# Lower halves of the experts' second weights computed ahead of the expert part and kept in DRAM

## The chip, the cores and the metric

The kernel runs on one core of a Trainium2 chip. The metric is the time of one execution on the device in microseconds (us); a version is judged by the median of its runs. A profile is one further execution with the hardware profiler on.

## What is computed

Three stages follow one another. The reference, cut to what matters here:

```python
a = exp(phi - max); a = a / sum(a)                       # memory slots, softmax over the sequence
k_m, v_m = a^T k, a^T v                                  # 8 x 8 heads, 32 slots of 64
x = softmax(q k_m^T / 8) v_m                             # 4608 tokens, 512 wide
x = max(x @ w1, x @ w2, x @ w3) @ w_out                  # 512 -> 768 -> 512
logits = x @ w_gate                                      # 8 experts
# tokens in order of their best logit take an expert, each expert takes at most 576 tokens
for e in range(8):
    h = maximum(x[mask_e] @ moe2_w1[e], 0)               # 512 -> 1024
    out[mask_e] = h @ moe2_w2[e]                         # 1024 -> 512
```

## The kernel before

TensorE multiplies each pair of matrices as three products of rounded float32 numbers: every operand is split in a high part (a rounded copy, made by ScalarE) and a low part (what the copy lost, made by a subtraction on VectorE or GpSimd), and high times high, high times low and low times high are added up in PSUM. The page's names are PE (TensorE), ACT (ScalarE), DVE (VectorE), POOL (GpSimd) and SP (the sync engine, which here issues nearly all loads and stores).

The first part works on four units of two batches each (1152 tokens). A unit has the attention, then `layer1` (L588 to L606: 72 steps of six products into one of three `acc` buffers in PSUM; the first of each three steps is read out by ACT, L604, the other two by DVE, L606), then `layer2` (L646 to L676, written to the DRAM tensor `x2s`). The weights of layer 1 are folded with the unit's `v_m` by `fold` (L560 to L584) from pieces `wr` that SP loads (L554). The order of unit 0 is a list written by hand (`ORDER`); in the units 1 to 3 the loop at the end of the kernel (L1208 to L1235) emits one step of `layer1` or `layer2` after another and lets the object `flow` put the steps of the next unit's attention between them. Layer 2 of the last six tiles of unit 2 and of all of unit 3 is put off into the stretch behind the units. `consts` (L1101) builds some thirty small tables for the routing, in a pool `route`, as steps of `flow`; in the kernel before it is called near the end of unit 0 (entry `X` of the list), so that its instructions run at the start of unit 1.

The second part takes the experts one after another. For each, routing finds the 576 tokens: small instructions on DVE with small products on PE between them, six digits of a search and then `close`, `ties`, `places` and `index` (L740 to L945), emitted through `flow` in the midst of the matmuls of the expert before. POOL gathers the tokens (`xg`, L988), PE transposes them, `l1` (L1023 to L1039, 16 steps of twelve products of 288 columns) makes the hidden layer, which ACT (L1038) and DVE (L1039) read out, and `l2` (L1048 to L1071) makes the output, which POOL scatters. The expert's weights come through four buffers `wa` of 512 KB, loaded by SP at the expert's number. `split1` (L1006) splits a first weight: `ah` by ACT (L1010), `al` by POOL (L1011). `split2` (L1014) splits an eighth of the second weight: `bh` by ACT (L1020), `bl` by POOL (L1021). So POOL makes 64 pieces of `al` and 64 of `bl`, each a subtraction of 128 x 512 numbers with both inputs in SBUF; the pieces of `bl` are emitted in the second half of an expert's `l1`.

All engines run their own instructions in the order in which they are emitted; a DMA that SP issues waits in that order too.

Of the kernel before, what the change touches and what calls it, by code (L numbers as in the profile page):

```python
# [77 lines left out]
def staged(f):  # L78

    def whole(*x):  # L80
        for _ in f(*x):
            pass
    whole.stages = f
    return whole
# [57 lines left out]
def moe_kernel(tc, q, k, v, phi, w1, w2, w3, w_out, w_gate, m_w1, m_w2, out):  # L142
# [15 lines left out]
    with ExitStack() as ctx:  # L158
        def pool(name, bufs=1, **kw):
            return ctx.enter_context(tc.tile_pool(name=name, bufs=bufs, **kw))  # L160
# [384 lines left out]
                G.tensor_tensor(wol[:, x, :DM], dst, woh[:, x, :DM].bitcast(F32), op=OP.subtract)  # L545

        halves = [(u, i, a) for u in range(NU) for i in range(NF) for a in range(2)]
        WR = 4  # L550
# [83 lines left out]
        @staged  # L634
        def split_h(u, t, c):
            hT = st["hT", u][:, 3 * c:3 * c + 3, 128 * t:128 * t + 128]
            hh = wp.tile([128, 3, 128], F32R, name="hh", bufs=3)
            hl = wp.tile([128, 3, 128], F32R, name="hl", bufs=3)
            st["h", u, t, c] = hh, hl
            A.activation(hh, hT, AF.Copy)  # L640
            yield
            V.tensor_tensor(hl, hT, hh.bitcast(F32), op=OP.subtract)
# [335 lines left out]
        def done(j):  # L978
            if j == 1:
                free[0] += 1  # L980
                wload()
# [31 lines left out]

        def split2(ph, m):  # L1014
            h, j = divmod(m, 2)
            if m == 0:
                st["w2"] = [mp.tile([128, FE // 128, DM], F32R, name=s, bufs=1) for s in ("bh", "bl")]
            r = st["raw", ph, "b", h][:, j]
            hi, lo = (x[:, m] for x in st["w2"])
            A.activation(hi, r, AF.Copy)  # L1020
            G.tensor_tensor(lo, r, hi.bitcast(F32), op=OP.subtract)  # L1021
            done(j)

        def l1(ph, m, h, k):
            xh, xl = st["xT"]
# [74 lines left out]

        def consts():  # L1101
            nonlocal before, onesb, row, rowb, lanef, vals, em8, em8b, me8, thr0, times, OH, reach, some, number, part, remR, asg, ucap, upper, lower, code, where, zero, Lm, am8, me, rp
            unit0.close()
            rp = pool("route", side="right")
            later = Later(V=V, G=G)

# [75 lines left out]
        for u in range(NU):  # L1182
            if u == 0:
                table = dict(lp=lambda b: load_phi(0, b), lpr=lambda: load_phr(0), lk=lambda n: more(load_kv, kvs),
                             lkr=lambda: load_kvr(0), ld=lambda n: load_d("w"), lo=lambda n: load_d("o"),
                             lq=lambda n: more(load_q, qs), lg=load_g, c=staged(lambda n: conv.stages("w", *divmod(n, 2))),
                             d=staged(lambda n: conv.stages("o", n)), g=gate_a, G=gate_b, X=consts, H=lambda *x: split_h(*x), M=layer2,
                             L=staged(lambda i, b, h, w: layer1.stages(0, i, b, h, w)))
                for n in range(2):
                    attT_steps(n)  # L1190
                    steps = dict(att_steps(n), T=st["T", n], f=staged(lambda i, g, n=n: fold.stages(n, i, g)))
                    table.update({"1" * n + x: f for x, f in steps.items()})
                live = {}
                for x in ORDER.split():
                    name, *x = x.replace("!", "").split(".")
                    x = tuple(int(y) for y in x)
                    f = table[name]
                    if name[-1] == "f" and (name, x) not in live:

                        for y in live:  # L1200
                            if y[0][-1] == "f":
                                for _ in live[y]:
                                    pass
                    if hasattr(f, "stages"):
                        next(live.setdefault((name, x), f.stages(*x) if (name, x) not in live else None), None)
                    else:
                        f(*x)
            else:  # L1208
                if u + 1 < NU:
                    flow.add(att_steps(u + 1))  # L1210
                    flow.spread(2.9 * 4 * NF)
                for i in range(NF):
                    for n in range(4):
                        for w in range(3):
                            flow.main(lambda: main1(u, i, n, w), 0.75 + 0.5 * (w == 0))
                flow.flush()
            if u == NU - 1:
                last_logits(u, NF - 1)
                last_logits2(u)
                break  # L1220
            if u == 0:
                continue
            flow.add(attT_steps(u + 1))

            nt = NT if u < NU - 2 else 3
            flow.spread(4.0 * nt)
            for t in range(nt):
                for i in range(NF):
                    if (t, i) in ((0, 3), (2, 3)):
                        fold(u + 1, 0, t // 2)  # L1230
                    flow.main(lambda: layer2(u, t, *divmod(i, 3)), 0.67)
            flow.flush()
            if u == NU - 2:
                attention.close()
                hp = pool("last", side="right")  # L1235
        phase1.close()
        mp = pool("moe")
# [39 lines left out]
        for ph in range(E):  # L1277
            more_ = ph + 1 < E
            runs = [(m, h) for m in range(FE // 128) for h in range(2)]
            if ph == 0:  # L1280

                runs[1:3] = runs[2:0:-1]
                for t in range(3):
                    x_steps(0)[t][0]()
            for n, (m, h) in enumerate(runs):
                if h == (ph == 0) and m + 2 < FE // 128:
                    split1(ph, m + 2)
                if m >= 4:
                    split2(ph, 2 * (m - 4) + h)
                for k in range(4):  # L1290
                    flow.main(lambda: l1(ph, m, h, k), 0.37)
                if ph == 0 and n < 2:
                    x_steps(0)[n + 3][0]()
            gathered = 0
            for t in range(5):
                if t in (1, 2):
                    half(ph, t - 1)
                for m in range(FE // 128):
                    if more_ and not gathered and (("si", ph + 1) in st and t or (t, m) == (3, 0)):
                        ready(ph + 1)  # L1300
                        gathered = t + 1
                    if more_ and (t, m) in ((3, 2), (3, 6)):
                        split1(ph + 1, m // 4)
                    flow.main(lambda: l2(ph, t, m), 0.65 if t < 4 else 0.43)
                    at = (0, 1, 2, 3, 4) if gathered < 4 else (1, 3, 5, 6, 7)
                    if more_ and t == 4 and m in at:
                        x_steps(ph + 1)[at.index(m)][0]()
# [25 lines left out]
```

## Time and profile before

| | before |
|---|---|
| median of 3 runs | 1166.09 us (1165.29 to 1168.97) |
| the profiled execution | 1170.43 us, its span 1168.7 us |
| PE busy | 1067.4 us (91% of the span) |
| DVE busy | 679.3 us (58%) |
| ACT busy | 397.2 us (34%) |
| POOL busy | 334.7 us (29%) |
| bytes moved by DMA | 127.75 MB, 109 GB/s over the span |

Unit 0 ends at 219 us, unit 1 at 357 us, unit 2 at 466 us and unit 3 at 546 us after the span's start; the first expert's products begin at 631 us. Shares of the whole span mix these stages, so the rows further down are taken by stage. A row that says what an engine waited for names the instruction that came last.

### The profile page before, as it was taken

The page shows a single profiled execution, that of the slowest core. Times are in us where ns is not written, and L with a number is a line of the kernel's source. Part 1 is how long each engine was busy: PE and PEld are TensorE (multiplying, and loading weights), DVE is VectorE, ACT ScalarE, POOL GpSimd, SP SyncE. Part 2 cuts the span into 40 slices and gives each one's busy share as a digit, 9 for nine tenths or more (in the row PEclk, how much of TensorE's full clock was granted, in tenths as well). Part 3 has the DMA queues.
Part 4 walks back from the last instruction along what each step waited for, and adds up shares of the span by engine and source line. Part 5 has one row for each costly group of instructions (what it writes and reads, how often), then busy time and mean ns, then how long its engine had stood idle before and what let it go on. Part 6 is the DMA issues. An engine that isn't in the chain of part 4 may idle for free.

```text
span 1168.7 us, 21288 instructions
## 1 busy us (share of the span) xinstructions
PE 1067.4 (91%) x8426; PEld 909.2 (78%) x8426; DVE 679.3 (58%) x1690; ACT 397.2 (34%) x879; POOL 334.7 (29%) x361
## 2 busy tenths in 40 slices
PE   4688999999999999999996898998989789899996
PEld 3477799878998888777775778887777777779895
DVE  6798844764636456434573768677694865822120
ACT  2454344424343334223332323242231412324240
POOL 2123210120101001000003545535454424556462
PEclk8799999999999999999997999999989989899999
DMA  9964545337211521200132332423232222333311
GB/s 289 314 203 141 171 120 170 96 105 226 86 69 59 154 78 46 76 16 10 55 127 77 108 113 60 140 69 119 78 120 91 80 66 91 109 113 115 111 59 40
DMA packets 103763, 127.75 MB, mean 109 GB/s; under 512 B 18928, under 2 KB 79344, under 8 KB 103664
## 3 DMA queue, kind: packets, MB, share of 16 engines
q1 hardware_dynamic: 95184, 102.80, 28.7%
q0 software_dynamic: 5888, 18.88, 5.1%
q10 hardware_dynamic: 2592, 4.72, 1.1%
q8 instruction: 66, 1.08, 0.4%
q14 instruction: 33, 0.27, 0.1%
HBM read 102.78 MB, written 23.59 MB: 108 GB/s over the span
## 4 chain that ended last, share of the span: by engine, by line
PE 35%; DVE 11%; issue 3%; POOL 2%; ACT 1%; another core or an unknown queue 1%; DMA 0%; POOLq 0%
PE acc L1036 12%; PE acc L1059 12%; PE acc L667 5%; PE acc L1063 2%; DVE reach L739 1%; PE tr L1000 1%; PE fold L755 1%; DVE hT L1039 1%; POOL bl L1021 1%; PE fold L939 1%; DVE gs L801 0%; DVE gx L804 0%; ACT hT L1038 0%; DVE wol L1003 0%
## 5 line engine op out<-in xcount | busy, mean ns | idle before, releaser
L600 PE MATMUL acc<-ah,Wh 128*128 128x288 f32 x576 | 180.6, 313 | 4.9 <-DVE hT L606 4.2
L1059 PE MATMUL acc<-bh,hT 128*128 128x512 f32 x512 | 173.0, 406 | 6.3 <-DVE hT L1039 6.3
L1036 PE MATMUL acc<-woh,ah 128*128 128x288 f32 x512 | 163.9, 320 | 10.0 <-DVE hT L1039 8.9
L600 PE MATMUL acc<-ah,Wl 128*128 128x288 f32 x576 | 169.7, 295 | 1.2 <-DVE Wl L584 1.2
L600 PE MATMUL acc<-al,Wh 128*128 128x288 f32 x576 | 169.9, 295 | 0.0
L1036 PE MATMUL acc<-wol,ah 128*128 128x288 f32 x512 | 158.1, 309 | 0.2
L1036 PE MATMUL acc<-woh,al 128*128 128x288 f32 x512 | 156.9, 306 | 0.0
L600 PEld LDWEIGHTS acc<-ah,Wh 128*128 128x128 f32 x576 | 108.1, 188 | 36.8 <-DVE hT L606 16.1
L606 DVE TENSOR_TENSOR hT<-hT,acc 128x288 f32<-128x288 f32 x192 | 85.8, 450 | 79.7 <-PE acc L600 72.0
L1059 PEld LDWEIGHTS acc<-bh,hT 128*128 128x128 f32 x512 | 97.6, 191 | 29.2 <-DVE hT L1039 7.0
L1036 PEld LDWEIGHTS acc<-woh,ah 128*128 128x128 f32 x512 | 102.6, 200 | 22.4 <-DVE hT L1039 10.4
L600 PEld LDWEIGHTS acc<-ah,Wl 128*128 128x128 f32 x576 | 108.1, 188 | 1.4 <-DVE Wl L584 1.4
L600 PEld LDWEIGHTS acc<-al,Wh 128*128 128x128 f32 x576 | 108.3, 188 | 0.1
L1038 ACT ACTIVATE hT<-acc 128x288 fp32r<-128x288 f32 x128 | 52.7, 412 | 151.0 <-PE acc L1036 141.5
L1011 POOL TENSOR_TENSOR al<-wa,ah 128x512 fp32r<-128x512 f32 x64 | 83.9, 1318 | 69.4 <-ACT ah L1010 69.0
L1036 PEld LDWEIGHTS acc<-wol,ah 128*128 128x128 f32 x512 | 102.7, 201 | 1.0 <-DVE wol L1003 0.7
L1036 PEld LDWEIGHTS acc<-woh,al 128*128 128x128 f32 x512 | 102.7, 201 | 0.0
L1059 PE MATMUL acc<-bl,hT 128*128 128x512 f32 x256 | 101.8, 398 | 0.0
L1021 POOL TENSOR_TENSOR bl<-wa,bh 128x512 fp32r<-128x512 f32 x64 | 85.7, 1364 | 34.3 <-ACT bh L1020 34.1
L1039 DVE SCALAR_TENSOR_TENSOR hT<-acc,hT 128x288 fp32r<-128x288 f32 x128 | 56.6, 453 | 64.5 <-ACT hT L1038 64.0
L988 POOL DMA_INDIRECT xg<-x2s,gi x40 | 41.0, 1025 | 179.9 <-DVE some L763 168.2
L1067 ACT ACTIVATE o<-acc 128x512 f32<-128x512 f32 (+1 forms) x40 | 23.9, 598 | 198.3 <-PE acc L1059 141.4
(263 smaller groups left out, 2076.6 us busy)
## 6 DMA issues: line engine op xcount, KB each, us to landing
wa<-in_moe_w_dram SPq DMA_DIRECT2D x64, 512.0 KB, 3.6
wr<-ws SPq DMA_DIRECT2D x36, 384.0 KB, 3.0
dw<-in_moe_w_dram SPq DMA_DIRECT2D x36, 256.0 KB, 4.7
q<-in_q_dram SPq DMA_DIRECT2D x7, 1024.0 KB, 5.5
kv<-in_k_dram SPq DMA_DIRECT2D x27, 256.0 KB, 4.3
kv<-in_v_dram SPq DMA_DIRECT2D x27, 256.0 KB, 4.6
ws<-wr SPq DMA_DIRECT2D x12, 384.0 KB, 2.9
x2s<-xs ACTq DMA_DIRECT2D x18, 256.0 KB, 2.0
```

What stands on the lines that cost most here:

```text
L600: PE.matmul(p, x[:, b, g, f], y[:, g, c], start=(n == 0), stop=(n == 5))
L606: V.tensor_tensor(o, o, p, op=OP.max)
L667: PE.matmul(p, x[:, j], y[:, i, width * a:width * a + width], start=(i == 0 and m == 0), stop=(i == NF - 1 and m == 2))
L988: G.indirect_dma_start(out=x[:n], out_offset=None, in_=x2s, in_offset=bass.IndirectOffsetOnAxis(ap=gi[:n, t:t + 1], axis=0))
L1011: G.tensor_tensor(lo, r, hi.bitcast(F32), op=OP.subtract)
L1021: G.tensor_tensor(lo, r, hi.bitcast(F32), op=OP.subtract)
L1036: PE.matmul(p, x[:, k], y[:, k, c], start=(k == 0 and i == 0), stop=(k == 3 and i == 2))
L1038: A.activation(hh[:, m, c], p, AF.Relu)
L1039: V.scalar_tensor_tensor(hl[:, m, c], p, 0.0, hh[:, m, c].bitcast(F32), op0=OP.max, op1=OP.subtract)
L1059: PE.matmul(p, x[:, m, c], y[:, m], start=(m == 0 and i == 0), stop=(m == K - 1 and i == 2))
L1063: PE.matmul(p, st["hx", m // 4][:, m % 4], y[:, m], start=(m == 0 and y is bh), stop=(m == K - 1 and y is bl))
L1067: A.activation(o[:n], p[:n], AF.Copy)
```

## The change

The low parts `bl` of all eight experts' second weights, 32 quarters of 512 KB, are made in the units 1 and 2 and stored to a new DRAM tensor `wl2`. `ahead_step` is called after each main step of these units and goes through seven positions per quarter n: at position 0 the first half of the quarter n (a copy on ACT, L563, and a subtraction on POOL, L564) and the store of quarter n - 1 on SP (L568); at position 3 the second half of n; at position 5 the load of quarter n + 1 on SP (L555). What 216 calls don't reach is emitted at once when unit 2 ends. In the expert part `split2` keeps the copy `bh` alone, and `load2` loads a quarter of `bl` straight to its place (L1056), at the steps 3, 5, 7 and 9 of `l1`. The raw second weight is still loaded for `bh`. The loads and the working buffers (`pw`, `pl`) need the room in SBUF in which the route pool stood, so the tables of `consts` are made at the start of unit 3.

```diff
+        wl2 = dp.tile([E, 4, 128, 2 * DM], F32, name="wl2")
+        ahead = [(e, h) for e in range(E) for h in range(4)]
+
+        def ahead_load(n):
+            if n < len(ahead):
+                e, h = ahead[n]
+                st["pw", n] = pw = qp.tile([128, 2, DM], F32, name="pw", bufs=2)
+                SP.dma_start(pw, m_w2[e, FE // 4 * h:FE // 4 * (h + 1), :].rearrange("(k p) f -> p k f", p=128))
+
+        def ahead_part(n, j):
+            if n >= len(ahead):
+                return
+            if j == 0:
+                st["pl", n] = qp.tile([128, 2, DM], F32R, name="pl", bufs=3)
+            w, x = st["pw", n][:, j], st["pl", n][:, j]
+            A.activation(x, w, AF.Copy)
+            G.tensor_tensor(x, w, x.bitcast(F32), op=OP.subtract)
+
+        def ahead_store(n):
+            if 0 <= n < len(ahead):
+                SP.dma_start(wl2[ahead[n]], st["pl", n].bitcast(F32).rearrange("p k f -> p (k f)"))
+
+        def ahead_step():
+            n, k = divmod(st["ahead"], 7)
+            st["ahead"] += 1
+            if k == 0:
+                ahead_part(n, 0)
+                ahead_store(n - 1)
+            elif k == 3:
+                ahead_part(n, 1)
+            elif k == 5:
+                ahead_load(n + 1)
...
         def split2(ph, m):
             h, j = divmod(m, 2)
-            if m == 0:
+            A.activation(st["w2"][0][:, m], st["raw", ph, "b", h][:, j], AF.Copy)
+            done(j)
+
+        def load2(ph, h):
+            if h == 0:
                 st["w2"] = [mp.tile([128, FE // 128, DM], F32R, name=s, bufs=1) for s in ("bh", "bl")]
-            r = st["raw", ph, "b", h][:, j]
-            hi, lo = (x[:, m] for x in st["w2"])
-            A.activation(hi, r, AF.Copy)
-            G.tensor_tensor(lo, r, hi.bitcast(F32), op=OP.subtract)
-            done(j)
+            SP.dma_start(st["w2"][1][:, 2 * h:2 * h + 2].bitcast(F32).rearrange("p k f -> p (k f)"),
+                         wl2[bass.ds(st["e", ph], 1), h].rearrange("o p f -> p (o f)"))
...
         def consts():
...
-            unit0.close()
             rp = pool("route", side="right")
...
-                             ..., X=consts, ...
+                             ..., X=unit0.close, ...
...
+                if u == 1:
+                    between = ctx.enter_context(ExitStack())
+                    qp = between.enter_context(tc.tile_pool(name="ahead", bufs=1, side="right"))
+                    st["ahead"] = 0
+                    ahead_load(0)
...
                             flow.main(lambda: main1(u, i, n, w), 0.75 + 0.5 * (w == 0))
+                            if u < NU - 1:
+                                ahead_step()
...
                     flow.main(lambda: layer2(u, t, *divmod(i, 3)), 0.67)
+                    ahead_step()
             flow.flush()
             if u == NU - 2:
+                while st["ahead"] < 7 * (len(ahead) + 1):
+                    ahead_step()
+                between.close()
                 attention.close()
+                consts()
                 hp = pool("last", side="right")
...
                 if h == (ph == 0) and m + 2 < FE // 128:
                     split1(ph, m + 2)
+                if n in (3, 5, 7, 9):
+                    load2(ph, n // 2 - 1)
                 if m >= 4:
                     split2(ph, 2 * (m - 4) + h)
```

The order of the instructions moves at three places. The order of PE is the same but for the attention steps between the products of unit 1.

On POOL, in the second of the eight experts: `xg` is the gather, `al` and `bl` are the low parts. Before, from the scatter of the expert ahead to the first scatter of this one:

```order
L1071 DMA out_dram<-o,si 4608x512
L1011 TENSOR_TENSOR al<-wa,ah 128x512 x5
L1021 TENSOR_TENSOR bl<-wa,bh 128x512 x2
L1011 TENSOR_TENSOR al<-wa,ah 128x512
L1021 TENSOR_TENSOR bl<-wa,bh 128x512 x6
L1070 MEMSET spacer 1x1
```

and with the change:

```order
L1106 DMA out_dram<-o,si 4608x512
L1045 TENSOR_TENSOR al<-wa,ah 128x512 x6
L1105 MEMSET spacer 1x1
```

Eight subtractions have left the place; the six of `al` stand where they stood.

On SP, where unit 2 ends and unit 3 begins (`x2s` is the store of a layer 2 tile, `wr` a load for a fold, `pw` a load and `wl` a store of a quarter). Before:

```order
L676 DMA x2s<-xs 128x512 x2
L554 DMA wr<-ws 128x768
L676 DMA x2s<-xs 128x512
L554 DMA wr<-ws 128x768 x6
```

and with the change:

```order
L710 DMA x2s<-xs 128x512
L568 DMA wl_100<-pl 128x1024
L588 DMA wr<-ws 128x768
L710 DMA x2s<-xs 128x512
L555 DMA pw<-in_moe_w_dram 128x2x512
L568 DMA wl_100<-pl 128x1024 x2
L588 DMA wr<-ws 128x768 x6
```

The load of the last quarter now stands behind the store of unit 2's last tile, and the last two stores behind it.

On DVE, at the same place (`hl` is a low part in layer 2 of unit 2, `Wl` one of a fold, `hT` the reading out of a `layer1` step, and L135 are the tables). Before:

```order
L642 TENSOR_TENSOR hl<-hT,hh 128x384
L584 TENSOR_TENSOR Wl<-fold,Wh 128x384 x2
L606 TENSOR_TENSOR hT<-hT,acc 128x288 x4
```

and with the change:

```order
L676 TENSOR_TENSOR hl<-hT,hh 128x384
L135 TENSOR_SCALAR before<-Lm 128x128
L135 MEMSET onesb 128x128
L135 CAST rowb<-row 128x128
L618 TENSOR_TENSOR Wl<-fold,Wh 128x384 x2
L640 TENSOR_TENSOR hT<-hT,acc 128x288
L135 CAST lanef<-lane 128x1
L640 TENSOR_TENSOR hT<-hT,acc 128x288
```

The first table stands ahead of the first reading out of unit 3. Its input `Lm` is filled by POOL, behind POOL's subtractions of the last quarter, and lies where the buffers `pw` and `pl` lay, so it also waits for the last store of `wl2` to land.

## Rows read from the trace of the kernel before

**Rows 1.** Busy time by stretch: us, engines' busy us, TensorE clock, DMA share, GB/s.

```profile
219.00:313.00 94.00, 91.19 (x913) 79.44 (x913) 55.72 (x140) 32.88 (x80) 8.76 (x11) 1.00 0.44 130
219.00:466.00 247.00, 242.11 (x2308) 212.34 (x2308) 140.13 (x323) 92.72 (x228) 22.30 (x26) 1.00 0.33 101
630.00:1052.00 422.00, 381.98 (x2652) 326.20 (x2651) 282.51 (x786) 124.95 (x254) 201.74 (x211) 0.95 0.30 96
1052.00:1107.00 55.00, 54.92 (x330) 48.87 (x328) 11.46 (x23) 20.68 (x42) 31.66 (x35) 1.00 0.38 120
```

**Rows 2.** What PE waited for, 630 to 1052 us: total us, times, longest.

```profile
PE acc L1036 <- DVE hT L1039: 8.9, 6, 4.9
PE acc L1059 <- DVE hT L1039: 6.3, 3, 4.3
PE fold L877 <- DVE lastb L858: 6.3, 4, 2.8
PE fold L840 <- DVE part L812: 5.8, 2, 3.0
```

**Rows 3.** DVE in order of time, 926 to 930 us: start, us, instruction.

```profile
926.45 1.33 DVE L907 SCALAR_TENSOR_TENSOR pos<-scan,off,mem 128x36 f32<-128x36 f32 x1
...
929.05 1.21 DVE L911 TENSOR_SCALAR lo<-pi 128x36 int32<-128x36 int32 x1
```

**Rows 4.** POOL in order of time, 926 to 934 us.

```profile
926.43 1.30 POOL L1011 TENSOR_TENSOR al<-wa,ah 128x512 fp32r<-128x512 f32 x1 [3.77 <-ACT ah L1010]
927.68 2.54 POOL L1021 TENSOR_TENSOR bl<-wa,bh 128x512 fp32r<-128x512 f32 x2
930.18 1.30 POOL L1011 TENSOR_TENSOR al<-wa,ah 128x512 fp32r<-128x512 f32 x1
931.43 2.59 POOL L1021 TENSOR_TENSOR bl<-wa,bh 128x512 fp32r<-128x512 f32 x2
```

**Rows 5.** Single lines of DVE: shortest, median and longest ns, first and last start.

```profile
L856 DVE TENSOR_TENSOR_SCAN scan<-tie,zero x7: 232/1193/1228, 589.9 to 993.5; 128x36 f32<-128x36 f32 x7
L1039 DVE SCALAR_TENSOR_TENSOR hT<-acc,hT x128: 434/457/459, 635.5 to 1133.2; 128x288 fp32r<-128x288 f32 x128
L642 DVE TENSOR_TENSOR hl<-hT,hh x72: 495/553/1412, 152.7 to 612.0; 128x384 fp32r<-128x384 f32 x72
```

**Rows 6.** Busy time by stretch, six stretches at a lower clock: the first and the sum.

```profile
726.00:734.00 8.00, 7.05 (x33) 6.91 (x34) 6.85 (x31) 2.12 (x5) 2.92 (x3) 0.57 0.42 133
...
sum 37.00, PE 33.20 PEld 30.75 DVE 27.57 ACT 7.24 POOL 9.91; mean PE 5.53 PEld 5.12 DVE 4.60 ACT 1.21 POOL 1.65
```

**Rows 7.** Groups by line: count, busy us, mean ns, idle before.

```profile
L1021 POOL TENSOR_TENSOR bl<-wa,bh 128x512 fp32r<-128x512 f32 x64 | 85.7, 1364 | 34.3 <-ACT bh L1020 34.1 <-DVE lastb L858 0.3
L1010 ACT ACTIVATE ah<-wa 128x512 fp32r<-128x512 f32 x64 | 39.0, 622 | 0.0
```

**Rows 8.** End of unit 2: SP, ACT, DVE and PE in order of time.

```profile
467.25 0.32 SPq L676 DMA_DIRECT2D x2s<-xs  x1
467.47 0.41 ACT L604 ACTIVATE hT<-acc 128x288 f32<-128x288 f32 x1 [0.25 <-PE acc L600]
468.79 1.02 DVE L584 TENSOR_TENSOR Wl<-fold,Wh 128x384 fp32r<-128x384 f32 x2 [2.17 <-ACT Wh L576]
471.41 0.29 PE L600 MATMUL acc<-ah,Wh 128*128 128x288 f32 x1
```

**Rows 9.** DMA issues by line: count, KB each, median us to landing.

```profile
wa<-in_moe_w_dram SPq DMA_DIRECT2D x64, 512.0 KB, 3.6
kv<-in_v_dram SPq DMA_DIRECT2D x27, 256.0 KB, 4.6
ws<-wr SPq DMA_DIRECT2D x12, 384.0 KB, 2.9
```

**Rows 10.** Unit 1: SP's issue of a fold's load, and ACT's next reading out.

```profile
232.96 0.32 SPq L554 DMA_DIRECT2D wr<-ws  x1
235.69 0.41 ACT L604 ACTIVATE hT<-acc 128x288 f32<-128x288 f32 x1 [1.91 <-PE acc L600]
```

More of the change, by code (lines that the diff above doesn't have):

```diff
@@ L1186, in moe_kernel @@
                              lq=lambda n: more(load_q, qs), lg=load_g, c=staged(lambda n: conv.stages("w", *divmod(n, 2))),
-                             d=staged(lambda n: conv.stages("o", n)), g=gate_a, G=gate_b, X=consts, H=lambda *x: split_h(*x), M=layer2,
+                             d=staged(lambda n: conv.stages("o", n)), g=gate_a, G=gate_b, X=unit0.close, H=lambda *x: split_h(*x), M=layer2,
                              L=staged(lambda i, b, h, w: layer1.stages(0, i, b, h, w)))
```

## The prediction

> **What bounds the kernel now.** I read the busy time by stretch first, then what PE waited for in the slow stretch, then DVE and POOL beside each other in time, and last the order at the places where instructions move. Up to the end of unit 2 PE is the bound: it is busy 242 of the 247 us of the units 1 and 2, at the full clock of 2.4 GHz, while POOL works 22 us and ACT 93 us [rows 1]. The experts with routing are another stage. In the 422 us from 630 on PE is busy 382 us and idle 40 us, and its mean granted clock is 0.95; an expert without routing, from 1052 to 1107, has PE busy all the time at full clock [rows 1]. So what the change can win lies in those 40 us and in that clock.
>
> Four kinds of waits hold 27.3 us of the idle time (8.9 + 6.3 + 6.3 + 5.8), all ended by DVE [rows 2]: for a routing result, or for a reading out of `acc` that stands behind routing instructions in DVE's queue. DVE is late there because its small instructions last far longer than their work. An instruction on 36 numbers per partition takes 1.33 or 1.21 us [rows 3] in the stretch in which POOL makes `al` and `bl` back to back, 1.3 us each [rows 4]. The scan of `close` takes 0.23 us at its shortest and 1.19 us at the median [rows 5]. The reading out of `acc`, which has one input in PSUM, takes 434 to 459 ns whatever POOL does [rows 5]. I read this as DVE waiting, in instructions with all inputs in SBUF, until the running POOL instruction ends. The Trainium skill says the same ("SBUF — State Buffer", section "Who interferes with whom": a VectorE instruction with two SBUF inputs contends with a GpSimd instruction that reads SBUF, the one that starts first keeps the port, and one with at most one SBUF input outside the two-port modes doesn't contend); the rows agree, and no sum rests on the rule.
>
> **Gain in the expert part.** Sixty-four subtractions `bl` leave POOL, 85.7 us of its time [rows 7], and they stand in the half of `l1` in which the waits of group 2 arise. Of six POOL instructions in the stretch shown, four are `bl` and two `al` [rows 4]; `al` stays. I take two thirds of the 27.3 us: 18.2 us. The waits also cost clock: behind them lie six stretches, 37 us together, where the granted clock is 0.57 (once 0.66), which is the level of 1.2 GHz most of the time. PE is busy 33.2 us in them [rows 6], so (33.2 - 4.4) x 0.43 + 4.4 x 0.34 = 13.9 us go to the clock. Two thirds again: 9.3 us. Together 27.5 us. The lower bound is the two longest waits alone, 4.9 and 4.3 us [rows 2], two thirds of them and of a clock stretch of 3.0 us (7.05 x 0.43) for each: 10 us. The upper bound is all of it, 41 us. I stay at two thirds since it is counted from instructions in the stretch where the waits are.
>
> The added loads of `bl` cost nothing here: 16.8 MB in 480 us are 35 GB/s where 96 GB/s take a DMA share of 0.30 [rows 1]. The last of the four is issued six `l1` steps ahead of `l2`, some 10 us (sixteen such steps are about half of the 55 us of an expert without routing [rows 1]), and a quarter lands in about 3.6 us, as `wa` does [rows 9]. On SP the `wa` loads behind them wait for splits of the same steps. `bh` on ACT is unchanged. If routing became faster than PE's order, nothing more would be won: the steps stand at fixed places among PE's products.
>
> **Cost at the end of unit 2.** The load of the last quarter is issued behind the store of unit 2's last tile, at 467.25 + 0.32 = 467.6 us [rows 8], and lands at 467.6 + 3.6 = 471.2 [rows 9]. The 15 calls left over then put two copies on ACT ahead of its first reading out of unit 3: 2 x 0.62 us [rows 7], which moves that one from 467.47 [rows 8] to 472.4. POOL subtracts behind each copy, 1.3 us each, until 474.5. SP then stores; 512 KB should land in about 3.6 us (384 KB take 2.9 [rows 9]): 478.2. Only then may POOL fill `Lm`, and DVE's first table waits for that: 478.7. Behind it on DVE stand two `Wl` of 1.02 us [rows 8] and the first reading out, 0.45 us [rows 5]: 480.5 with the semaphores. PE has three `acc` buffers; its sixth accumulation needs the one that DVE gives back, and started at 471.41 [rows 8]. It is 9.1 us late. The idle time should also bring the lower clock, 3.0 us as in the stretch from 726 [rows 6]: 12 us. Bounds: 5 us if the tables don't wait for the store, so that only ACT's 4.9 us count; 15 us if the store is slower and the tables keep DVE behind. The tables themselves are the same work as at the start of unit 1, where they leave; I cost the move at nothing else.
>
> **Cost in the units 1 and 2.** ACT gets 64 copies of 0.62 us = 40 us, on 93 of 247 us; POOL 64 x 1.3 = 84 us, on 22; both have room [rows 1, 7]. DMA gets 33.6 MB in 247 us, 136 GB/s. At 0.30 for 96 GB/s that adds 0.42 to a share of 0.44 in the first 94 us of unit 1 [rows 1]: heavy, not full. What can hurt is order. SP issues a fold's load only when that fold is done; a quarter's load behind it is then late. At 232.96 SP issues such a load [rows 10]; the next quarter's load follows at 233.3 and lands at 236.9, the copy ends at 237.6, and the reading out that ACT began at 235.69 is 1.9 us late. Two further accumulations give PE about 2 us to cover that (unit 3 makes its 72 in 80 us). From the order, four of the 31 quarters before the last have their load that close behind a fold, some ten more are nearly so. I take 1 us for the four and 0.1 us for the ten: 5 us. Below: 0, if the buffers cover all. Above: 15, if DMA load makes all landings 2 us longer. POOL's subtractions can also hold DVE here as they did there: `hl`, with both inputs in SBUF, has taken 1412 ns against a median of 553 [rows 5]. Most of DVE's instructions here, the readings out and `Wl`, have an input in PSUM and didn't suffer [rows 5], so I add nothing for it and make it a rival.
>
> **The sum.** - 27.5 + 12 + 5 = - 10.5 us. Against the profiled execution, 1170.4, that is 1159.9 us. It was 4.3 us slower than the median of the runs, 1166.1; so 1155.6 us is predicted for the median. What a measurement of this kernel can tell from no change is about 0.3%, 3.5 us.
>
> **The rivals.**
> *Half the relief.* Routing instructions that no longer meet `bl` may meet `al`, which comes earlier once `bl` is gone from the queue, or DVE's own work may be the bound (it is busy 282 of 422 us [rows 1]). For it: two of six POOL instructions stay. Against: `al` waits for ACT, not for POOL's queue (3.77 us idle for `ah` [rows 4]). With 13.8 us instead of 27.5: 1169 us, between no change and slower.
> *Late quarters (slower).* ACT's queue is the place: a copy that waits for its load holds up the readings out of `layer1`. The price is 2 us for each quarter that is late by more than the buffers cover. For it: the margin in the case above is nothing, and kv halves already take 4.6 us to land in a stretch of the same kind [rows 9]. Against: most loads are issued 3 to 7 us ahead. It decides once loads land after 6 us rather than 3.6, since the ten near cases then count too: 14 x 2 = 28 us in place of 5, 1179 us.
> *Contention moved.* The 64 subtractions cost DVE in the new place: up to 1.41 - 0.55 = 0.86 us each time an `hl` meets one [rows 5]. There are 24 of them in the units 1 and 2; if each met one and each held up PE, that would be 20 us: 1176 us. Against: `hl` is made two groups ahead of its use. This is where the rule of the Trainium skill's page "SBUF — State Buffer" speaks against the change: as long as POOL makes the subtractions somewhere, the port is taken somewhere.
> *No relief at all.* If DVE's long instructions are not POOL's doing through `bl`, only the costs stay: 1166 + 17 = 1183 us. The shortest and the median of the scan speak against it [rows 5].
>
> **How the numbers follow.** The forecast gets 0.68 and by its bounds 1143 to 1163; half the relief 0.17, late quarters 0.08, contention moved 0.04, no relief 0.03. The second case lies around 1169: of its 0.17 I put 0.11 within 0.3% of before (1162.6 to 1169.6) and 0.03 on either side. Faster is then 0.68 + 0.03 = 0.71, the same 0.11, slower 0.08 + 0.04 + 0.03 + 0.03 = 0.18. The range takes in the first two cases, 0.85 less what lies beyond their own bounds: 1143 to 1172 us.
>
> **What would show it.** In the changed profile: DVE's scan and the other small instructions of `close` and `places` back near 0.23 us where `bl` was; the four waits of group 2 down from 27 us to 9 or so, and the clock above 0.97 from 630 to 1052 us; a new idle time of PE of 8 to 10 us right behind the end of unit 2, ended by DVE; some waits of PE for ACT in the units 1 and 2, none above 2 us. It is wrong if the stage of the experts is not shorter by 15 us or more, or if the units 1 and 2 take over 10 us longer.

## The result and the profile after

| | before | with the change |
|---|---|---|
| median of 4 runs | 1167.53 us (1165.29 to 1171.28) | 1152.65 us (1150.29 to 1154.33) |
| ratio, 95% interval | | 0.9868 (0.9834 to 0.9902) |
| span of the profiled execution | 1168.7 us | 1152.5 us |

The change is 1.3% faster, 14.9 us between the medians; 10.5 us less and 1155.6 us were predicted. That the two agree is partly luck: the gain and the costs were both larger than I put them. The stages show it. Busy time by stretch, first of the kernel before, cut at the first product of each stage: unit 1, unit 2, `layer1` of unit 3, the late layer 2, the experts with routing (columns as in [rows 1]):

```profile
219.24:357.11 137.87, 134.77 (x1291) 121.12 (x1291) 75.69 (x186) 50.96 (x126) 11.14 (x13) 1.00 0.37 113
357.11:466.43 109.32, 107.53 (x1021) 91.37 (x1020) 64.86 (x138) 41.51 (x101) 11.15 (x13) 1.00 0.28 87
466.43:545.02 78.59, 78.45 (x664) 61.30 (x664) 31.20 (x70) 20.68 (x48) 0.00 (x0) 1.00 0.12 35
545.02:631.27 86.25, 75.90 (x447) 56.18 (x447) 53.81 (x182) 26.38 (x51) 7.35 (x7) 0.96 0.25 85
631.27:1052.81 421.54, 382.20 (x2653) 326.65 (x2654) 282.31 (x785) 124.35 (x253) 200.47 (x210) 0.95 0.30 95
```

The same stages of the changed kernel:

```profile
218.92:365.65 146.73, 138.43 (x1291) 124.34 (x1290) 80.90 (x158) 68.64 (x162) 58.48 (x49) 0.98 0.71 231
365.65:483.59 117.94, 111.03 (x1020) 94.36 (x1019) 65.90 (x137) 54.64 (x127) 44.09 (x39) 0.97 0.58 192
483.59:573.10 89.51, 82.42 (x664) 63.98 (x664) 34.97 (x99) 21.59 (x50) 4.29 (x9) 0.94 0.15 49
573.10:659.11 86.01, 75.83 (x447) 56.15 (x447) 53.75 (x182) 26.36 (x51) 7.32 (x7) 0.95 0.25 85
659.11:1036.73 377.62, 365.37 (x2653) 313.01 (x2653) 246.04 (x785) 124.37 (x253) 135.65 (x162) 0.99 0.42 140
```

Unit 1 grew by 8.9 us, unit 2 by 8.6, unit 3 by 10.9; the experts shrank by 43.9. With - 0.3 at the start and - 0.2 in the late layer 2 that makes - 16.0, against - 16.1 between the spans. Of the 17.5 us in the units 1 and 2 PE is idle for 10.3 (4.9 before, 15.2 now) and busy for 7.2 longer with the same products, since the granted clock, 1.00 before, is 0.98 and 0.97 now.

**The experts.** PE's 2653 products are the same, so the 43.9 us are idle time, 39.3 before (421.54 - 382.20) and 12.3 after, a gain of 27.1; and clock, 382.20 - 365.37 = 16.8 (granted clock 0.95 before, 0.99 after). What PE still waits for from 659 to 1037 us (total, times, longest), all but three shorter rows:

```profile
PE fold L789 <- DVE reach L773: 4.1, 6, 1.4
PE acc L1071 <- DVE hT L1074: 3.1, 3, 1.5
PE fold L911 <- DVE lastb L892: 1.3, 1, 1.3
PE acc L1094 <- DVE hT L1074: 1.3, 1, 1.3
```

The four waits of [rows 2], 27.3 us, are 5.7 us now (3.1 + 1.3 + 1.3; `part` is gone). `reach` stayed as it was, 4.2 us before.

**The units 1 and 2.** One quarter's path at its worst, on SP, ACT and PE in order of time (start, us, instruction, idle time before it):

```profile
297.08 0.39 SPq L555 DMA_DIRECT2D pw<-in_moe_w_dram  x1
...
303.49 0.63 ACT L563 ACTIVATE pl<-pw 128x512 fp32r<-128x512 f32 x1 [6.77 <-issue]
304.03 0.58 ACT L390 ACTIVATE qT<-tr 128x512 f32<-128x512 f32 x1
304.51 0.40 ACT L638 ACTIVATE hT<-acc 128x288 f32<-128x288 f32 x1
...
304.96 0.40 PE L634 MATMUL acc<-ah,Wh 128*128 128x288 f32 x1 [2.18 <-ACT hT L638]
```

SP issued the load behind four `rest` loads and a fold's load, it landed at 303.4, ACT stood still for 6.77 us, the reading out behind the copy came late, and PE with it. What PE waited for from 218.9 to 484 us (total, times, longest):

```profile
PE sc L342 <- DMA kv<-in_v_dram: 6.5, 3, 2.5
PE acc L634 <- ACT hT L638: 4.6, 5, 2.2
PE acc L634 <- DVE hT L640: 2.5, 3, 1.2
PE fold L701 <- DVE Wl L618: 1.3, 1, 1.3
```

Before, `kv` cost PE 1.6 us here and no wait was ended by ACT. What the engines of all instructions on `pw` waited for, then the page's rows of the new DMAs (KB each, median us to landing):

```profile
its engine sat idle before it (us, times) until:
  ACT pl L563: 149.4, 53
  DMA pw<-in_moe_w_dram: 26.1, 9
  issue: 24.0, 8
```
```profile
pw<-in_moe_w_dram SPq DMA_DIRECT2D x32, 512.0 KB, 5.1
wl<-pl SPq DMA_DIRECT2D x32, 512.0 KB, 4.5
bl<-wl SPq DMA_DIRECT2D x32, 512.0 KB, 5.1
```

The first row is POOL waiting for the copy; the other two are ACT's copies, 50 us in 17 places, 16 in the units 1 and 2 and one at the end of unit 2, all of it for a load (under "issue" too the copies begin within 0.2 us of a landing, as the one shown). A quarter took 5.1 us to land, not 3.6.

**The end of unit 2.** The last quarter's load, the copies, the subtractions, and the first table, on SP, ACT, POOL, DVE and PE:

```profile
484.42 0.32 SPq L710 DMA_DIRECT2D x2s<-xs  x1
484.79 0.43 SPq L555 DMA_DIRECT2D pw<-in_moe_w_dram  x1
...
489.25 1.15 ACT L563 ACTIVATE pl<-pw 128x512 fp32r<-128x512 f32 x2 [4.86 <-DMA pw<-in_moe_w_dram]
...
489.96 2.51 POOL L564 TENSOR_TENSOR pl<-pw,pl 128x512 fp32r<-128x512 f32 x2 [5.45 <-ACT pl L563]
495.58 0.24 POOL L135 IOTA Lm<- 128x128 int32 x1 [3.12 <-DMA wl<-pl]
...
495.86 0.24 DVE L135 TENSOR_SCALAR before<-Lm 128x128 bf16<-128x128 int32 x1 [10.94 <-POOL Lm L135]
...
490.75 0.59 PE L634 MATMUL acc<-ah,Wh 128*128 128x288 f32 x1 [3.63 <-ACT hT L638]
493.04 0.61 PE L634 MATMUL acc<-ah,Wh 128*128 128x288 f32 x1 [0.50 <-ACT hT L638]
497.64 0.61 PE L634 MATMUL acc<-ah,Wh 128*128 128x288 f32 x1 [2.79 <-DVE lanef L135]
```

This is the chain of the prediction, link by link (each within 0.9 us of it, counted from the unit's first product). The sixth accumulation of unit 3 starts 14.05 us behind the unit's first (497.64 - 483.59), before 4.98 ([rows 8]: 471.41 - 466.43): 9.1 us late, as forecast. Three waits before it, two ended by ACT and one by DVE, are 6.9 us of that, slower products the rest. Behind the wait the granted clock is at the lower level, 1.2 GHz:

```profile
494.00:500.00 6.00, 3.21 (x14) 2.86 (x14) 3.61 (x16) 0.00 (x0) 0.86 (x6) 0.50 0.33 106
```

### The profile page after: what moved, and what is told of

Read it like the earlier page. It is cut to its first block, busy times and chain, and to the rows that moved or that the text cites. A ratio compares the mean times of both kernels' runs of the same rounds, so it can differ in the third digit from the quotient of the medians.

```text
span 1152.5 us, 21555 instructions
## 1 busy us (share of the span) xinstructions
PE 1062.0 (92%) x8426; PEld 904.6 (78%) x8426; DVE 652.9 (57%) x1690; ACT 428.9 (37%) x943; POOL 334.0 (29%) x361
## 5 line engine op out<-in xcount | busy, mean ns | idle before, releaser
L634 PE MATMUL acc<-ah,Wh 128*128 128x288 f32 x576 | 184.4, 320 | 16.8 <-ACT hT L638 9.4
L1071 PE MATMUL acc<-woh,ah 128*128 128x288 f32 x512 | 158.2, 309 | 4.2 <-DVE hT L1074 3.1
L1071 PE MATMUL acc<-wol,ah 128*128 128x288 f32 x512 | 153.2, 299 | 0.2
L1071 PE MATMUL acc<-woh,al 128*128 128x288 f32 x512 | 152.3, 297 | 0.0
L564 POOL TENSOR_TENSOR pl<-pw,pl 128x512 fp32r<-128x512 f32 x64 | 84.0, 1316 | 149.5 <-ACT pl L563 149.4
L634 PEld LDWEIGHTS acc<-al,Wh 128*128 128x128 f32 x576 | 110.9, 193 | 0.1
L1071 PEld LDWEIGHTS acc<-woh,ah 128*128 128x128 f32 x512 | 97.9, 191 | 7.4 <-DVE hT L1074 3.8
L1106 POOL DMA_INDIRECT out_dram<-o,si x40 | 40.8, 1021 | 215.9 <-ACT o L1102 163.8
L1071 PEld LDWEIGHTS acc<-wol,ah 128*128 128x128 f32 x512 | 97.8, 191 | 1.0 <-DVE wol L1037 0.7
L1071 PEld LDWEIGHTS acc<-woh,al 128*128 128x128 f32 x512 | 98.1, 192 | 0.0
```

Of the source, the lines that this page charges most:

```text
L564: G.tensor_tensor(x, w, x.bitcast(F32), op=OP.subtract)
L634: PE.matmul(p, x[:, b, g, f], y[:, g, c], start=(n == 0), stop=(n == 5))
L1071: PE.matmul(p, x[:, k], y[:, k, c], start=(k == 0 and i == 0), stop=(k == 3 and i == 2))
L1106: s = G.indirect_dma_start(out=out, out_offset=bass.IndirectOffsetOnAxis(ap=st["si", ph][:n, t:t + 1], axis=0), in_=o[:n], in_offset=None)
```

## The experiments

All stages as above, in us, each from one profiled execution; each ratio is against the kernel before on the same chip, with its 95% interval.

| kernel | unit 1 | unit 2 | unit 3 | experts | median | ratio |
|---|---|---|---|---|---|---|
| before | 137.9 | 109.3 | 78.6 | 421.5 | | 1 |
| the change | 146.7 | 117.9 | 89.5 | 377.6 | 1152.7 | 0.9868 (0.9834 to 0.9902) |
| one_eighth | 139.9 | 108.8 | 78.8 | 377.3 | 1127.9 | 0.9664 (0.9627 to 0.9702) |
| pool_again | 147.0 | 115.2 | 90.5 | 420.8 | 1190.3 | 1.0187 (1.0146 to 1.0227) |
| pool_iota | 146.8 | 115.1 | 90.2 | 383.4 | 1159.9 | 0.9928 (0.9902 to 0.9955) |
| dma_only | 139.9 | 113.9 | 86.3 | 378.7 | 1141.8 | 0.9778 (0.9739 to 0.9817) |
| load_early | 142.2 | 113.4 | 85.4 | 377.3 | 1144.2 | 0.9798 (0.9760 to 0.9836) |
| early6 | 142.5 | 113.4 | 78.8 | 376.8 | 1135.2 | 0.9740 (0.9713 to 0.9766) |
| spread | 139.4 | 110.5 | 83.7 | 377.5 | 1133.7 | 0.9722 (0.9700 to 0.9745) |
| spread_late | 139.5 | 110.9 | 78.8 | 379.2 | 1131.3 | 0.9660 (0.9630 to 0.9689) |
| al_on_act | 147.3 | 117.1 | 89.8 | 365.7 | 1142.7 | 0.9790 (0.9763 to 0.9818) |
| al_on_dve | 138.9 | 111.4 | 78.8 | 370.7 | 1123.6 | 0.9593 (0.9563 to 0.9623) |
| before_bl_dve | 137.6 | 109.1 | 78.6 | 400.2 | 1149.7 | 0.9851 (0.9813 to 0.9890) |
| before_both_dve | 137.3 | 109.3 | 78.6 | 388.6 | 1137.0 | 0.9746 (0.9709 to 0.9783) |

The units 1 to 3 of pool_again, pool_iota and al_on_act are those of the change, and yet unit 2 took 115.1 to 117.9 us in these four. Differences of two or three us between single rows of the table are therefore no finding by themselves.

### Where the costs are: one_eighth

```diff
...
-        ahead = [(e, h) for e in range(E) for h in range(4)]
+        ahead = [(e, h) for e in range(1) for h in range(4)]
...
-                         wl2[bass.ds(st["e", ph], 1), h].rearrange("o p f -> p (o f)"))
+                         wl2[0, h])
```

> Only the four quarters of expert 0 are made ahead, in the first 28 steps of unit 1, and every expert loads these as its bl; seven eighths of the low parts are left out. The expert part is as in the change, the added work of the units 1 and 2 is nearly gone, the tables of consts still stand at the start of unit 3. If the 28 us that the units 1 to 3 grew by come from the added work: unit 1 back from 146.7 us to about 140, unit 2 from 118 to about 109, unit 3's layer1 from 89.5 to 79 to 82, the experts with routing stay at 378 us, the total is about 1127 us. If the move of the tables costs by itself, unit 3 stays near 89 us and the total is about 1137 us. If the gain of the experts came from anything the making ahead does to them, they would change too.

The costs vanish, but for 2.0 us in unit 1, where the four quarters are made, and the gain stays: they come from the added work. Moving the tables costs nothing where no quarter is left over: unit 3 takes 78.8 us with them at its start, 78.6 without.

### What the gain is: pool_again and pool_iota

```diff
...
+            bx = mp.tile([128, DM], F32R, name="bx", bufs=1)
+            G.tensor_tensor(bx, r, hi.bitcast(F32), op=OP.subtract)
```

> The change, with POOL also making the subtraction in split2 again, into a spare tile that nothing reads. Theory that POOL's subtraction itself holds DVE's instructions: the scan is back near 1.2 us in the median, the experts with routing take 415 to 425 us instead of 378, the clock there is 0.95 again, the total is about 1190 us. Rival, that the experts gained because PE waits for a bl no more or because the loads take its place: they stay at 378 to 385 us and the total is 1153 to 1160 us.

With POOL's subtractions back, read by nobody, the experts take as long as before the change, to 0.7 us, and none of PE's waits there is ended by POOL or by a load. Busy time from 658.6 us on, then of pool_iota:

```profile
658.59:1079.38 420.79, 379.87 (x2652) 324.54 (x2653) 280.77 (x785) 124.20 (x253) 200.81 (x210) 0.95 0.37 125
```
```profile
660.05:1043.43 383.38, 365.63 (x2653) 312.29 (x2653) 252.77 (x785) 124.36 (x253) 188.86 (x258) 0.99 0.41 138
```

DVE's busy time is what tells it: 282.3 us before, 246.0 with the change, 280.8 here, for the same 785 instructions. My own sign, the scan's median, failed: it was 0.233 us here too, since only two of the seven scans began while POOL was in a subtraction. Those two took 1.22 and 1.35 us, the other five 0.23. The first of the two, beside POOL:

```profile
818.66 1.26 POOL L1053 TENSOR_TENSOR bx<-wa,bh 128x512 fp32r<-128x512 f32 x1
818.78 1.22 DVE L890 TENSOR_TENSOR_SCAN scan<-tie,zero 128x36 f32<-128x36 f32 x1
```

The median of a few instructions is no gauge of a contention; the sum over the stage is.

```diff
+            bx = mp.tile([128, DM], I32, name="bx", bufs=1)
+            for _ in range(2):
+                G.iota(bx, pattern=[[1, DM]], base=0, channel_multiplier=0)
```

> The change, with two iotas of 128 x 512 integers on POOL in the place of each bl subtraction of the kernel before: they read nothing in SBUF and write 2 KB per partition each, some 0.6 to 0.8 us (the iota of 128 x 128 took 0.24 us), so that POOL is about as busy as with the subtraction. Theory that DVE is held by a POOL instruction that reads two operands in SBUF: the scan stays at 0.23 us in the median, the experts with routing at 378 to 384 us, total 1153 to 1159 us. Rival, that any busy POOL holds DVE's instructions, or that al behind it in POOL's queue is what comes late: 400 us or more, total 1175 us or more, as in pool_again.

POOL is busy 188.9 us, nearly as with the subtractions (200.8), yet the experts lose 5.8 us instead of 43.2. (The iotas, unlike the subtractions, wait for no copy of ACT, so they stand in the same order but not at the same times, and each lasts 0.56 us.) A busy POOL is not the cause, nor POOL's queue; an instruction that reads its operands in SBUF is. What remains is seen in two lines of DVE in this kernel (shortest, median, longest ns): the scan, with two inputs, is untouched, an instruction with one input and a constant is held.

```profile
L890 DVE TENSOR_TENSOR_SCAN scan<-tie,zero x7: 232/232/233, 618.8 to 989.0; 128x36 f32<-128x36 f32 x7
```
```profile
L945 DVE TENSOR_SCALAR lo<-pi x8: 182/325/592, 625.3 to 1010.7; 128x36 int32<-128x36 int32 x8
```

Four of the seven scans ran beside an iota, as this one:

```profile
689.69 0.56 POOL L1053 IOTA bx<- 128x512 int32 x1
689.93 0.23 DVE L890 TENSOR_TENSOR_SCAN scan<-tie,zero 128x36 f32<-128x36 f32 x1
```

The scan and the `tensor_scalar` agree with the Trainium skill ("SBUF — State Buffer", section "Who interferes with whom"): two-input instructions of VectorE meet GpSimd's reads but not its writes, while a `tensor_scalar` that runs in a two-port mode needs the whole shared pair. Which mode these ran in no row shows.

### What the making ahead costs: dma_only and load_early

dma_only drops the copy and the subtraction from `ahead_part` and stores `pw` itself, with five buffers:

```diff
...
-            w, x = st["pw", n][:, j], st["pl", n][:, j]
-            A.activation(x, w, AF.Copy)
-            G.tensor_tensor(x, w, x.bitcast(F32), op=OP.subtract)
...
-                SP.dma_start(wl2[ahead[n]], st["pl", n].bitcast(F32).rearrange("p k f -> p (k f)"))
+                SP.dma_start(wl2[ahead[n]], st["pw", n].rearrange("p k f -> p (k f)"))
```

> The change without the copies on ACT and the subtractions on POOL in the units 1 and 2: a quarter is loaded into one of five buffers and stored as it came (the split of the second weights is left out). Theory that ACT's queue is the place (a copy that waits for its load holds up the readings out): the units 1 and 2 go back to 138 to 141 and 109 to 112 us, the total is about 1128 us. Rival, that the DMA load is the place (kv and fold loads land later): they stay at 144 to 147 and 115 to 118 us, with PE waiting for kv, and the total is 1145 to 1152 us.

Neither theory alone: of the 17.5 us in the units 1 and 2, 6.6 stay with the transfers alone (139.9 + 113.9 - 137.9 - 109.3), and there PE waits 6.4 us for `kv`, 4.8 more than before. The rest, 11 us, belongs to the copies and subtractions with their waits for loads. Unit 3 is still 7.7 us late, without any copy: the tables wait for the last store alone.

load_early issues each load one quarter earlier (three buffers `pw`, and `pl` in five halves, for the room):

```diff
...
-                ahead_load(n + 1)
+                ahead_load(n + 2)
...
```

> The change with each quarter's load issued a quarter (seven steps, some 9 us) earlier, three buffers pw, and pl in half tiles that are stored one by one. Theory that late quarters block ACT: ACT no longer waits for pw in the units 1 and 2 (38 us of waits before), PE's waits there fall from 14.5 us to 6 or less, the end of unit 2 no longer waits for the last load, the total is about 1135 us. Rival, DMA load or POOL: PE's waits stay above 10 us and the total within 4 us of 1152.7.

The units 1 and 2 cost 8.5 us instead of 17.5: the 9 us (6 to 9 by the four rows that share these units) are what late quarters did through ACT's queue. ACT waits for no load there any more, and PE's wait for ACT fell from 4.6 us to 0.5. All of PE's waits there are 9.9 us, between what the theory and the rival asked for. What stays is again near the 6.6 us of the transfers, with the same waits for `kv`, 6.5 us. The total is 9 us above what I expected, since unit 3 gained only 4.1 us: the tables still start only when the last store has landed. So does now ACT's first reading out, which in the change ran 5 us before that store landed; here it begins 0.2 us behind the landing at 483.2 us:

```profile
483.43 0.41 ACT L638 ACTIVATE hT<-acc 128x288 f32<-128x288 f32 x1 [4.63 <-issue]
```

### Versions that avoid the costs: early6, spread, spread_late

early6 is load_early with six steps per quarter instead of seven, so that nothing is left over:

```diff
-            n, k = divmod(st["ahead"], 7)
+            n, k = divmod(st["ahead"], 6)
...
-            elif k == 5:
+            elif k == 4:
...
```

> The loads a quarter earlier as in load_early, and six steps per quarter instead of seven, so that all 32 quarters are stored before unit 2 ends. If the 6.8 us that unit 3 still grew by in load_early (layer1 85.4 us against 78.6) come from the quarters left over at the end of unit 2, unit 3's layer1 is back at 79 to 80 us; the denser loads cost the units 1 and 2 one to two us more: total about 1139 us. If they come from the tables of consts, unit 3 stays at 85 us and the total is 1144 to 1147 us.

Unit 3 is back at 78.8 us, and the denser loads cost the units 1 and 2 next to nothing more. So the leftover quarters were the whole cost at the end of unit 2.

spread makes 23 quarters in the units 1 and 2 and 9 in unit 3, in the room that the attention's buffers leave there:

```diff
+        LAST = 23
+        st["late"] = False
...
-            n, k = divmod(st["ahead"], 7)
+            n, k = divmod(st["ahead"], 7 if st["late"] else 9)
+            n += LAST if st["late"] else 0
...
-                            if u < NU - 1:
-                                ahead_step()
+                            ahead_step()
...
-                while st["ahead"] < 7 * (len(ahead) + 1):
-                    ahead_step()
...
+                qp = between.enter_context(tc.tile_pool(name="ahead2", bufs=1))
+                st["ahead"], st["late"] = 0, True
...
```

> The loads a quarter earlier, 23 quarters at nine steps each in the units 1 and 2 and the last 9 at seven steps each in unit 3, where the DMA share was 0.12 and POOL idle. Theory that what is left of the cost in the units 1 and 2 is DMA load in the attention's stretches (kv late): the units 1 and 2 cost 4 to 6 us in place of the 8.5 us of load_early, unit 3's layer1 takes 79 to 81 us, the total is about 1134 us, 1127 us being the floor that one_eighth showed. Rival, that new quarters in unit 3 hold up its readings out as they did at its start: unit 3 at 85 us or more, the total 1142 us or more.

The units 1 and 2 cost 2.8 us, better than I put it. Unit 3 loses 5.1, between the two forecasts: ACT waits 2.65 us for its first quarter in the unit's first six microseconds, and DVE 3.73 us for a table (`lane`) that POOL fills behind that quarter's subtraction. spread_late starts there fourteen steps later (`st["ahead"] = -14`) at six steps per quarter:

> As spread, but in unit 3 the first load comes eight steps and the first copy fourteen steps after its start, at six steps per quarter. Theory that spread's 5.1 us in unit 3 come from its first 20 us, where the readings out, the tables and the first copies meet: unit 3's layer1 takes 79 to 80 us, the total is about 1129 us. Rival, that any quarter in unit 3 costs it (DVE beside POOL, ACT's queue): it stays at 83 to 84 us and the total at 1133 us.

Unit 3 takes 78.8 us with nine quarters made in it: its start was the place, not the quarters. The total is 2 us more than expected, most of it in unit 0 (unit 1 starts 1.7 us later than in spread) and in the experts, 379.2 us.

### What al still costs, and who else could subtract: al_on_act, al_on_dve, before_bl_dve, before_both_dve

```diff
-            G.tensor_tensor(lo, r, hi.bitcast(F32), op=OP.subtract)
+            A.activation(lo, r, AF.Copy)
```

> The change with al made by a second copy on ACT instead of POOL's subtraction (the low part of the first weights is left out, the high part stands in its place), so that POOL makes no subtractions in the expert part at all. If the al that remain still cost PE time: DVE's stretched instructions (26 us beside al) are gone, the experts with routing take 362 to 368 us instead of 378, the total is about 1139 us. If what idle time remains is DVE's own chain of routing, they stay at 374 to 378 us and the total within 4 us of 1152.7.

The 64 subtractions `al` that the change leaves on POOL cost 12.0 us more; of PE's waits in this kernel's experts the largest group is 1.3 us, and `reach` is down to 1.0. The first 64 subtractions to leave POOL took 36.3 us off DVE's busy time (282.3 to 246.0) and gave 43.9; the other 64 took 24.2 (246.0 to 221.8) and gave 12.0. (The stage as cut here takes in 48 of the 64 pieces of `bl` and about as many of `al`.)

al_on_dve is spread_late with `al` made by DVE:

```diff
-            G.tensor_tensor(lo, r, hi.bitcast(F32), op=OP.subtract)
+            V.tensor_tensor(lo, r, hi.bitcast(F32), op=OP.subtract)
```

> As spread_late, with al in the expert part made by DVE instead of POOL. Theory that DVE is better off with 64 subtractions of some 0.6 us each (38 us) than with 26 us of stretch beside POOL's al, since nothing meets a POOL instruction then: the experts with routing take 366 to 372 us instead of 378, the total is about 1121 us. Rival, that DVE's queue, which then waits for ACT's copy ah ahead of readings out and of routing, is the worse place: 378 to 395 us, the total 1129 to 1146 us.

370.7 us and 1123.6 us: DVE is better off doing the work itself. It is the fastest kernel of this study, 4.1% below the kernel before. The last two put the same question to the kernel before, with that one letter changed in `split2`, and then in `split1` and `split2`:

> The kernel before, nothing made ahead, with bl made by DVE instead of POOL (al stays on POOL). If what the change won is the absence of POOL's bl, and DVE can carry 64 subtractions of some 0.6 us, the experts with routing take 378 to 390 us here too, without any cost in the units 1 to 3: total about 1128 to 1138 us, below the change. Rival, that DVE's queue, which then waits for ACT's bh ahead of readings out and of routing, takes the gain back: 400 us or more, total 1150 us or more.

> The kernel before with both al and bl made by DVE, so that POOL makes no subtractions in the expert part. From al_on_dve (371 us with al on DVE and bl loaded): if DVE has room for both, 371 to 385 us for the experts with routing and a total of 1117 to 1131 us; DVE would be busy some 280 us of these. Rival, that DVE's queue becomes the bound: 400 us or more and a total of 1146 us or more.

Both expected too much, and both beat what the change set out from. With `bl` alone on DVE the experts take 400.2 us, at the edge of the rival, and the total, 1149.7, is that of the change. With both it is 388.6 us and 1137.0 us: below the change, with nothing stored and nothing made ahead. DVE makes a piece in half of POOL's time (page rows of before_both_dve and of the change, count, busy us, mean ns):

```profile
L1021 DVE TENSOR_TENSOR bl<-wa,bh 128x512 fp32r<-128x512 f32 x64 | 43.7, 683 | 0.6
```
```profile
L1045 POOL TENSOR_TENSOR al<-wa,ah 128x512 fp32r<-128x512 f32 x64 | 83.8, 1316 | 86.9 <-ACT ah L1044 84.3
```

Its 87 us of subtractions are partly paid by the stretch that goes: DVE is busy 276.5 us in the experts, less than before the change.

## Why the prediction held, and where it didn't

**The bound** was read rightly: DVE held up by POOL's subtractions, PE waiting for it, the clock falling behind the waits. pool_again and pool_iota show that it is the subtraction's reading of SBUF. The scan's median, which I gave as a sign, came out as forecast (0.232 us) but tells nothing, since pool_again has it too.

**The gain in the expert part** was put at 27.5 us and was 43.9, above the upper bound of 41. The step that failed is "two thirds again". I took the share of `bl` among POOL's instructions for its share of the waits and of the clock. As a share of the delay it was near: `bl` made 36.3 of the 60.5 us of DVE's time that went with `bl` and `al`, 60%. Of the time of the stage that went with both it made 43.9 of 55.9 us, 79%. My reading, which no run shows by itself, is that a wait is what is left of a delay when the cover is used up: with half of the delay gone, the rest fits under the cover. The four waits lost 79% (27.3 to 5.7), the shorter rows that I hadn't counted lost another 5.5 us (27.1 - 21.6), and the clock gave back 16.8 us where I put 9.3: of the eight stretches at the lower level that begin between 631 and 1053 us (the six of [rows 6], and two at 996 and 1016) one is left, 3.4 us long. al_on_act agrees with that reading, 12 us for the second half. But no run takes `al` away and leaves `bl`; that `bl` simply stands where the waits arise, which the prediction gave as a reason, stays as a rival. "All of it" was no upper bound, as it held only the waits of [rows 2] and the clock of [rows 6].

**The cost at the end of unit 2** was put at 12 us, bounds 5 to 15, and was 10.9; the sixth accumulation came 9.1 us late as worked out, and what follows it cost 1.8 us more, where I put 3.0. The sign, 8 to 10 us of idle time ended by DVE, came only in part: it is 6.9 us, 4.1 ended by ACT (3.6 the longest) and 2.8 by DVE, and 4.0 of the 10.9 us are PE's products at the lower clock.

**The cost in the units 1 and 2** was put at 5 us, bounds 0 to 15, and was 17.5 (14.7 to 17.5 in the four kernels that share these units). The steps that failed: "lands at 236.9", 3.6 us behind its issue, where 5.1 were measured in the median, though the DMA share was 0.71 and 0.58, no more than I had reckoned with; and "four of the 31 quarters", where ACT stood waiting for 16 of them. I also priced the late quarters alone, not what a loaded DMA does to the transfers that were already there: 6.6 us by dma_only, with `kv` as its row. And I put the clock at nothing here, without a reason, while I counted it behind the waits of the other stages: 7.2 of the 17.5 us are PE's products at a granted clock of 0.98 and 0.97. "None above 2 us" was nearly right: 2.2 for ACT.

**The rivals.** Late quarters: it was there, at 9 us of its 28 (load_early). Contention moved: the subtractions did stretch `hl` (up to 1647 ns against [rows 5]'s 1412), but with the loads early all that is left in the units 1 and 2 is 8.5 us, 6.6 of it the transfers'. By that difference some 2 us are DVE's, which is no more than single rows scatter by. Half the relief and no relief fell: 43.9 us. The sign "the clock above 0.97 from 630 to 1052 us" held (0.99), "a stage shorter by 15 us" held, and "units 1 and 2 over 10 us longer", which I gave as a sign of being wrong, came true too: the sum was saved by a gain that was 16 us larger, against costs that were 11 us larger.

The loads of `bl` in the experts cost nothing that PE's waits show, as forecast: none is ended by them, at a DMA share of 0.42.

## What to carry to other kernels

Where one engine stretches another's instructions, remove the overlap before moving the work: a subtraction on the engine that suffers can be cheaper than the same one on the engine beside it, and needs no memory and no transfers. A delay's share of the waits is not its share of the delay: here the half that was taken away first was worth most, be it for the order or for its place. Work made ahead should be loaded two pieces early, end before the stage does, and lie where the DMA queues are empty; each of these was worth 5 to 10 us here.

## What the runs showed of the hardware that I had not expected

Loads of 512 KB don't land alike: `wa` took 3.8 us (3.6 before), `pw` 5.1 at a DMA share of 0.58 to 0.71, but `bl` 5.1 too, in the same stretch as `wa`, at 0.42; what makes `bl` slower wasn't tried. The `kv` loads' medians rose from 4.3 and 4.6 us to 4.8 and 5.2. An iota on POOL leaves DVE's two-input scan at 232 ns, where a subtraction on POOL stretches it to 1.2 us and more, but it stretches a `tensor_scalar` of 182 ns to 592. A subtraction of 128 x 512 numbers takes 0.68 us on DVE and 1.3 us on POOL.
